# Attention visits of two pairs at a time, on a three-bank PSUM tile, inside a feed-forward matmul stream

## The chip, the cores and the metric

The kernel runs on one core of one Trainium2 chip. The metric is the device time of one execution in microseconds (us). Each engine of the core runs its own list of instructions in order: TensorE (PE, with its weight loads as PEld), VectorE (DVE), ScalarE (ACT), GpSimd (POOL), and SyncE (SP), which here issues nearly all DMA.

## The reference

Eight batches of 576 tokens, eight heads of 64. Heads 0 to 3 attend to the last 32 positions ("local"), heads 4 to 7 to earlier positions with the same remainder by 32 ("strided"). The attention output, 576 x 512 for each batch, goes through a layer norm, two matrices with a ReLU between them, and a residual sum.

```
rel = pos[:, None] - pos[None, :]
mask_local = (rel >= 0) & (rel < 32)
mask_strided = (rel >= 0) & (pos[None, :] % 32 == pos[:, None] % 32)
attn = softmax(where(mask, q @ k.T / 8, -1e9)); attn = attn @ v
x = attn.transpose(0, 2, 1, 3).reshape(B, S, 512)
xn = (x - mean) / sqrt(var + 1e-6) * g_ln
out = x + relu(xn @ w_ch1) @ w_ch2
```

## The kernel before

The feed-forward part sets the rhythm. Tokens come in nine chunks of 512 (one for each batch, and one of the 8 x 64 tokens left over), and the hidden width in 16 slices of 128. One **step** is one chunk and one slice: `ffn1` (L560) runs 12 matmuls of 128x512 into one PSUM bank `ph` (L568, L572), after which ACT makes `hh` (the rounded ReLU, L576) and DVE makes `hl` (what the rounding left, L577); `ffn2` (L581) runs 12 matmuls that add the previous step's `hh` and `hl` into four banks `po` (L587). There are 144 steps, numbered from 0, in the order of `runs`: chunk 0 slices 0 to 7 (steps 0 to 7), chunk 1 (8 to 23), chunk 0 slices 8 to 15 (24 to 31), then chunks 2 to 8 (from step 32, 16 each). Early steps also split the weights into two parts; that ends with step 16.

Attention is worked off in between. A **pair** is two heads of one batch; pairs are numbered 0 to 31, four for each batch, alternately local (even) and strided (odd). A pair needs four pieces of TensorE work: scores `s_piece` (`sp`, L384 or L396), transposes of the weights `p_piece` (`pp`, L429), values `v_piece` (`av`, L443 or L452) and transposes of the result `x_piece` (`px`, L485). The two heads of a pair sit in rows 0-63 and 64-127 of the array, the output rows in column tiles of 32 (local) or 64 (strided); the profile counts two instructions for each such small fp32 matmul. The generator `pieces()` (L771) gives the pieces in order, and each `next(gen)` in the loop over steps is one **visit**: the piece's TensorE work goes between `ffn1` and `ffn2` of that step (or behind `ffn2`, third entry of `slots`). All pieces share one PSUM tile `a` of two banks, so a piece waits until the one before has been read out. From step 24 to 29 each step has two visits, later one, until the pairs are used up.

Between the pieces DVE adds the mask to the scores (`sm`, L403), takes the maximum (`mx`, L410), POOL subtracts it (L419), ACT takes the exponential (L424); after the values DVE divides by the sum of the weights, which comes out of a column of ones beside v (`den`, L458; `xo`, L464), and SP stores `xo`. After the last transposes ACT and DVE split the result into `xh` and `xl` (L502, L504), which `ffn1` of that batch's chunk reads. `turn()` (L764) has DVE transpose the next pair's q and k from `raw` (L361, L366) and SP load the raw rows of the pair after; it stands at the end of a step.

From step 17 on `ps_h` has two banks, which `ffn1` takes in turn (L562). PSUM has eight banks: four for `po`, two for `a`, one for `h`, one that belongs first to `ps_r` and from then on to `h`.

Of the kernel before, what the change touches and what calls it, by code (L numbers as in the profile page):

```python
# [20 lines left out]
def kernel(  # L21
# [46 lines left out]
    ps_r_ctx = ExitStack()  # L68
    ps_r = ps_r_ctx.enter_context(tc.tile_pool(name="ps_r", bufs=1, space=bass.MemoryType.PSUM))

# [107 lines left out]
    class Split:  # L178
# [44 lines left out]
        def column_mean(self, apart=False):  # L223
            if apart:
                self.mean = bank(f"cm{self.f}")[:, 0:P]
            else:
                self.mean = ps_h[0].tile([P, CH], F32, tag="h", name=f"cm{self.f}")[:, 0:P]
            nc.tensor.matmul(self.mean, mean, self.w[0][:, 0:P], start=True, stop=True)
# [18 lines left out]
    banks = [(ps_a, "a")]  # L247
    n_bank = [0]

    def bank(name):  # L250
        pool, tag = banks[n_bank[0] % len(banks)]
        n_bank[0] += 1
        return pool.tile([P, 1024], F32, tag=tag, name=name)

# [9 lines left out]
    class Pair:  # L264
# [45 lines left out]
        def t_rows(self):  # L310
            self.qt, self.kt = (qt_l, kt_l) if self.local else (qt_s, kt_s)
            ps = bank(f"t{self.id}").rearrange("p (c x) -> p c x", c=NR)
            pool, tag = ((ps_r, "r"), (ps_h[0], "h"))[self.local]
# [60 lines left out]
        def s_scores(self):  # L374
            ps = bank(f"sp{self.id}")
            nt = self.nt
            if self.local:
                w, mask = 64, mask_l
                sp = halves(ps, nt, w)
# [9 lines left out]
            else:  # L389
                w, mask = GS, mask_s  # L390
                sp = halves(ps, nt, w)
                for g in range(2 * NS):
                    t, c = divmod(g, 2)
                    for h in range(2):
# [4 lines left out]
                            start=True, stop=True, tile_position=(64 * h, 64 * c))  # L399

            self.sm = sms[int(self.local)]
            sm = self.sm[:, 0:nt, :, 0:w].rearrange("p t h x -> p h t x")
            nc.vector.tensor_tensor(  # L403
                out=sm, in0=sp, in1=mask.unsqueeze(1).unsqueeze(1).broadcast_to([P, 2, nt, w]),
                op=ALU.add)
            if self.local:
# [28 lines left out]
        def v_piece(self):  # L435
# [11 lines left out]
            else:  # L447
# [17 lines left out]
                out=xo[:, 0:nt].rearrange("p t h d -> p h t d"), in0=av[:, :, :, 0:D],  # L465
                in1=den.unsqueeze(3).broadcast_to([P, 2, nt, D]), op=ALU.mult)
            xov = xo.rearrange("p t h d -> p t (h d)")
            self.xov = xov
            if self.local:
                x_b = xd_l[self.b]  # L470
                nc.sync.dma_start(x_b[0:CH, cs].rearrange("(t p) c -> p t c", p=P), xov[:, 0:NT])
                nc.sync.dma_start(x_b[CH:S, cs], xov[0:REST, NT])
            else:
                x_b = xd_s[self.b].rearrange("(t c s) d -> c s t d", c=2, s=GS)
                for c in range(2):
                    nc.sync.dma_start(x_b[c, :, :, cs], xov[64 * c:64 * c + GS, 0:nt])

        def x_piece(self):

            xh, xl = x_t(self.b)  # L480
            cc = self.h0 // 2
            px = bank(f"px{self.id}")
            nt = NT if self.local else NS
            for t in range(nt):
                nc.tensor.transpose(px[:, P * t:P * (t + 1)], self.xov[:, t], ident)  # L485
            if self.local:
# [16 lines left out]
            for src, dst in parts:  # L503
                nc.vector.tensor_tensor(  # L504
                    out=dst(xl), in0=src, in1=dst(xh).bitcast(F32), op=ALU.subtract)

    def split_x(hi, lo, src):
# [49 lines left out]

    n_ffn1 = [0]

    def ffn1(c, f):  # L560
        xh, xl = xt[c]
        ph = ps_h[n_ffn1[0] % len(ps_h)].tile([P, CH], F32, tag="h", name=f"ph{c}_{f}")  # L562
        n_ffn1[0] += 1
        w1h, w1l = (w1s[f][:, i].rearrange("p (c f) -> p c f", c=NCC) for i in range(2))
# [104 lines left out]
    act, dve = nc.scalar.copy, nc.vector.tensor_copy  # L669
    idle = ps_h[0].tile([P, CH], F32, tag="h", name="idle")  # L670
    for i in range(12):
# [88 lines left out]
    def turned(i):  # L760
        if i < NP:
            todo.append(i)
# [8 lines left out]
    def pieces():  # L771

        pairs[NHP].p_piece()
        yield
        for i in range(NHP, NP):
            late = i == 2 * NHP - 1
            if i + 1 < NP and not late:
                pairs[i + 1].s_piece()
                if i + 2 != 2 * NHP:
                    turned(i + 2)  # L780
                yield
            pairs[i].v_piece()
            if i + 2 < NP:
                pairs[i + 2].load_v()
            yield
            if i + 1 < NP and not late:
                pairs[i + 1].p_piece()
                yield
            pairs[i].x_piece()
            if late:  # L790
                turned(i + 1)
            yield
            if late:
                pairs[i + 1].s_piece()
                turned(i + 2)
                yield
                pairs[i + 1].p_piece()
                yield

    gen = pieces()  # L800
    runs = [Run(0, 0, SPLIT), Run(1, 0, NFC), Run(0, SPLIT, NFC)]
# [21 lines left out]
    load = LOADED  # L823
    single = True

# [9 lines left out]
    for n, (r, f) in enumerate(steps):  # L835
        if f == r.f0:
            r.open()
        if load < NFC:
            w_load(load)
            load += 1  # L840
        if single and n > NFC and old is None:
            single = False
            ps_r_ctx.close()
            ps_h.append(ctx.enter_context(
                tc.tile_pool(name="ps_h1", bufs=1, space=bass.MemoryType.PSUM)))
        second = list(range(NT)) if prev is not None else []
        h = ffn1(r.c, f)
        if new and n:
            new.low(0)
# [38 lines left out]
        if old:  # L888
            old.two_parts(1)
        turn()  # L890
        following = prepare(n + 1)
# [48 lines left out]
```

## Time and profile before

| what | us |
|---|---|
| median of 3 runs (967.85, 967.9, 970.51) | 967.9 |
| the profiled execution | 971.69 |
| its span, first to last instruction | 969.9 |
| TensorE matmuls busy | 932.8 (96%) |
| VectorE busy | 388.5 (40%) |
| ScalarE, GpSimd busy | 222.2, 142.8 |

The busy share of TensorE counts matmuls that overlap, each as long as it is in flight, so it says that the engine hardly ever stands empty, not how much of it is needed. What a piece of work costs is read from the distance between two steps. The granted clock is the share of full speed that TensorE was given.

### The profile page before, as it was taken

How to read it: one execution, taken by the hardware profiler on the slowest of the kernel's cores; microseconds unless marked ns; L12 is line 12 of the kernel's file. 1: busy time of each engine (PE TensorE's matmuls, PEld its weight loads, DVE VectorE, ACT ScalarE, POOL GpSimd, SP SyncE). 2: the span in 40 equal slices, each digit the busy share in tenths (PEclk: the TensorE clock that was granted, in tenths of full speed). 3: DMA queues.
4: the chain of work that ended last, by engine and by line, in shares of the span. 5: the costliest groups of instructions: out<-in, count | busy, mean ns of one | idle time of the engine just before them, and what ended most of it. 6: DMA issues, size and time to landing. Idle time of an engine off the chain costs nothing.

```text
span 969.9 us, 19085 instructions
## 1 busy us (share of the span) xinstructions
PE 932.8 (96%) x8176; PEld 762.2 (79%) x8176; DVE 388.5 (40%) x681; ACT 222.2 (23%) x374; POOL 142.8 (15%) x180
## 2 busy tenths in 40 slices
PE   7678899999999999999999999999999999999996
PEld 6556688887788888888888888888888888888885
DVE  3557556444653344433443243335432331122112
ACT  2345557312121212121111121112111111110100
POOL 3246538410100000000100010001000000000000
PEclk8889999999999999999999999999999999999998
DMA  9986771143653233323342434243411121002001
GB/s 200 229 190 173 212 209 59 32 100 89 145 116 81 58 67 75 95 51 72 73 103 52 83 73 105 52 83 73 105 27 36 47 75 46 0 1 87 1 1 43
DMA packets 231971, 82.83 MB, mean 85 GB/s; under 512 B 184656, under 2 KB 222672, under 8 KB 231888
## 3 DMA queue, kind: packets, MB, share of 16 engines
q1 hardware_dynamic: 231360, 81.63, 36.4%
q8 instruction: 64, 1.05, 0.5%
q14 instruction: 19, 0.16, 0.0%
q10 hardware_dynamic: 528, 0.00, 0.0%
HBM read 61.08 MB, written 20.51 MB: 84 GB/s over the span
## 4 chain that ended last, share of the span: by engine, by line
PE 88%; DVE 4%; ACT 2%; issue 2%; SPq 1%; POOL 1%; DMA 1%; DVEq 0%; POOLq 0%; ACTq 0%
PE po L587 39%; PE ph L568 26%; PE ph L572 13%; PE pp L429 2%; PE px L485 2%; PE sp L396 1%; PE av L452 1%; PE av L443 1%; PE sp L384 1%; PE t L317 1%; DMA rows<-in_k_dram 1%; POOL sm L419 1%; DVE x L634 0%; DVE hl L577 0%; SPq L289 0%
## 5 line engine op out<-in xcount | busy, mean ns | idle before, releaser
L587 PE MATMUL po<-w,hh 128*128 128x512 f32 x1152 | 369.2, 402 | 0.0
L577 DVE SCALAR_TENSOR_TENSOR hl<-ph,hh 128x512 fp32r<-128x512 f32 x144 | 99.6, 691 | 500.4 <-ACT hh L576 500.4
L587 PEld LDWEIGHTS po<-w,hh 128*128 128x128 f32 x1152 | 208.3, 189 | 41.9
L568 PE MATMUL ph<-xh,w 128*128 128x512 f32 x576 | 226.8, 394 | 2.3 <-DVE hl L577 1.8
L587 PE MATMUL po<-w,hl 128*128 128x512 f32 x576 | 226.2, 393 | 0.0
L568 PE MATMUL ph<-xl,w 128*128 128x512 f32 x576 | 225.4, 391 | 0.0
L576 ACT ACTIVATE hh<-ph 128x512 fp32r<-128x512 f32 x144 | 85.9, 597 | 546.6 <-PE ph L572 546.6
L572 PE MATMUL ph<-xh,w 128*128 128x512 f32 x576 | 154.5, 390 | 0.0
L568 PEld LDWEIGHTS ph<-xh,w 128*128 128x128 f32 x576 | 108.9, 189 | 25.5 <-DVE hl L577 2.0
L587 PEld LDWEIGHTS po<-w,hl 128*128 128x128 f32 x576 | 108.5, 188 | 24.7
L568 PEld LDWEIGHTS ph<-xl,w 128*128 128x128 f32 x576 | 108.8, 189 | 22.4
L572 PEld LDWEIGHTS ph<-xh,w 128*128 128x128 f32 x576 | 108.4, 188 | 22.7
L419 POOL TENSOR_TENSOR sm<-sm,mx 128x640 f32<-128x640 f32 (+1 forms) x32 | 40.6, 1270 | 432.6 <-DVE mx L410 428.9
L546 POOL TENSOR_TENSOR rs<-rs,mhalf 128x1 f32<-128x1 f32 x36 | 19.7, 548 | 311.7 <-DVE rs L545 311.7
L424 ACT ACTIVATE sm<-sm 128x640 f32<-128x640 f32 (+1 forms) x32 | 23.8, 743 | 118.3 <-POOL sm L419 118.3
L504 DVE TENSOR_TENSOR xl<-px,xh 128x512 fp32r<-128x512 f32 (+2 forms) x48 | 30.0, 656 | 13.4 <-ACT xh L502 13.4
L429 PE MATMUL pp<-ident,sm 128*128 128x128 f32 x176 | 26.2, 285 | 6.2 <-DVE xo L464 3.6
L429 PEld LDWEIGHTS pp<-ident,sm 128*128 128x128 f32 x176 | 22.0, 147 | 11.7 <-issue 3.5
L502 ACT ACTIVATE xh<-px 128x512 fp32r<-128x512 f32 (+2 forms) x48 | 27.5, 648 | 7.2 <-PE px L485 6.5
L464 DVE TENSOR_TENSOR xo<-av,den 128x640 f32<-128x640 f32 (+1 forms) x32 | 28.5, 891 | 1.1
L432 ACT COPY pt<-pp 128x640 f32<-128x640 f32 (+1 forms) x32 | 23.9, 746 | 20.1 <-PE pp L429 17.7
L410 DVE TENSOR_REDUCE mx<-sm 128x10 f32<-128x640 f32 (+1 forms) x32 | 26.4, 824 | 2.1
(86 smaller groups left out, 601.1 us busy)
## 6 DMA issues: line engine op xcount, KB each, us to landing
s<-in_moe_w_ch_dram SPq DMA_DIRECT2D x32, 512.0 KB
out_dram<-x SPq DMA_DIRECT2D x32, 256.0 KB
raw<-in_q_dram SPq DMA_DIRECT2D x104, 72.0 KB
raw<-in_k_dram SPq DMA_DIRECT2D x104, 72.0 KB
xds<-xo SPq DMA_DIRECT2D x32, 162.0 KB
v_l<-in_v_dram SPq DMA_DIRECT2D x32, 144.0 KB
v_l<-in_v_dram SPq DMA_DIRECT2D x32, 136.0 KB
xdl<-xo SPq DMA_DIRECT2D x16, 256.0 KB
```

The source lines that it names most:

```text
L410: nc.vector.reduce_max(mx[:, :, 0:nt], sm, axis=AX.X)
L419: nc.gpsimd.tensor_tensor(out=sm, in0=sm, in1=mx[:, :, 0:nt].unsqueeze(3).broadcast_to([P, 2, nt, w]), op=ALU.subtract)
L429: nc.tensor.transpose(pp[:, P * t:P * (t + 1)], self.sm[:, t].rearrange("p h x -> p (h x)"), ident)
L432: nc.scalar.copy(out=self.pt[:, 0:self.nt].rearrange("p t x -> p (t x)"), in_=pp[:, 0:P * self.nt])
L464: nc.vector.tensor_tensor(out=xo[:, 0:nt].rearrange("p t h d -> p h t d"), in0=av[:, :, :, 0:D], in1=den.unsqueeze(3).broadcast_to([P, 2, ...
L502: nc.scalar.activation(out=dst(xh), in_=src, func=AF.Copy)
L504: nc.vector.tensor_tensor(out=dst(xl), in0=src, in1=dst(xh).bitcast(F32), op=ALU.subtract)
L568: nc.tensor.matmul(ph, w1h[:, cc], x[:, cc, :], start=(n == 0), stop=False)
L572: nc.tensor.matmul(ph, w1l[:, cc], xh[:, cc, :], start=False, stop=(cc == NCC - 1))
L576: nc.scalar.activation(out=hh, in_=ph, func=AF.Relu)
L577: nc.vector.scalar_tensor_tensor(out=hl, in0=ph, scalar=0.0, in1=hh.bitcast(F32), op0=ALU.max, op1=ALU.subtract)
L587: nc.tensor.matmul(run.po[i], hx[:, cs], w, start=(f == run.f0 and n == 0), stop=(f == run.f1 - 1 and n == 2))
```

## The change

From the third batch on (pair 8), two visits take the place of four. `scores_and_values(pv, p)` puts the values of pair `i` and the scores of pair `i + 1` in one visit; `weights_and_x(px, p)` puts the transposes of the result of pair `i` and of the weights of pair `i + 1` in another. Both use a PSUM tile `b` of three banks; the third comes from `ffn1`, which keeps a single bank `ph`. The two heads of a matmul pair are laid out in different banks.

The sum of the weights is no longer a column beside v but a `reduce_sum` over `sm` on DVE. Empty blocks are left out: 36 small matmuls instead of 40 for a local piece, 22 instead of 24 for a strided one. In exchange the mask addition takes two DVE instructions instead of one, and the division three.

`slots` now gives steps 19 and 21 one visit each, each of steps 24 to 31 one, and from step 32 to 110 every second step one. `turn()` moves, from step 17 on, from the end of the step to right behind `ffn1`. Steps 0 to 16 keep their order.

```diff
-    ps_a = ctx.enter_context(tc.tile_pool(name="ps_a", bufs=1, space=bass.MemoryType.PSUM))
-    ps_h = [ctx.enter_context(tc.tile_pool(name="ps_h", bufs=1, space=bass.MemoryType.PSUM))]
+    ps_h = ctx.enter_context(tc.tile_pool(name="ps_h", bufs=1, space=bass.MemoryType.PSUM))
...
+    def scores_and_values(pv, p):
...
+        for n in range(max(map(len, passes))):
+            both = [x[n] if n < len(x) else [] for x in passes]
+            for k in range(max(map(len, both))):
+                for x in both:
+                    if k < len(x):
+                        dst, at, by, pos = x[k]
+                        nc.tensor.matmul(dst, at, by, start=True, stop=True, tile_position=pos)
+        if p:
+            p.s_max(w, [(P, 0, last, a_s[:, :, :, 0:w]), (64, last, last + 1, b_s[0:64, :, :, 0:w])])
+            p.s_exp()
+        if pv:
...
+            pv.x_store(xo, slice(P * pv.n0, P * (pv.n0 + 1)), whole=False)
+
+    def weights_and_x(px, p):
...
+        k = -n_x % NT
+        for t, src in turns_p[:k] + turns_x + turns_p[k:]:
+            nc.tensor.transpose(ps[:, P * t:P * (t + 1)], src, ident)
+        if px:
+            px.x_parts(ps)
+        if p:
...
+            nc.vector.reduce_sum(p.den, p.smv, axis=AX.X)
...
+    def visits():
+
+        for i in range(2 * NHP - 1, NP):
+            p = pairs[i + 1] if i + 1 < NP else None
+            pv = pairs[i] if i >= 2 * NHP else None
+            scores_and_values(pv, p)
+            turned(i + 2)
+            if pv and i + 2 < NP:
+                pairs[i + 2].load_v()
+            yield
+            weights_and_x(pv, p)
+            yield
...
-            slots[n] = (int(8 < f < 14), 0, 0)
+            slots[n] = (int(f in (11, 13)), 0, 0)
         elif r is runs[2]:
-            slots[n] = (1, 0, int(f < 14))
+            slots[n] = (1, 0, 0)
         elif r.c + 1 < B:
-            slots[n] = (1, 0, 0)
+            slots[n] = (int(f % 2 == 0), 0, 0)
...
-        if single and n > NFC and old is None:
-            single = False
-            ps_r_ctx.close()
-            ps_h.append(ctx.enter_context(
-                tc.tile_pool(name="ps_h1", bufs=1, space=bass.MemoryType.PSUM)))
+        if n == NFC + 1:
+            assert old is None and next(gen, None) is None
+            gen = joint
+            first_ctx.close()
+            banks[:] = [(ctx.enter_context(
+                tc.tile_pool(name="ps_b", bufs=1, space=bass.MemoryType.PSUM)), "b")]
+            n_banks[0] = 3
         h = ffn1(r.c, f)
+        if gen is joint:
+            turn()
```

TensorE's list before, from the second visit of step 26 to the first of step 28: four visits, each between two groups of feed-forward matmuls (left out here). `sp` are scores, `pp` and `px` transposes, `av` values; the x at the end counts the matmuls.

```order
L396 MATMUL sp_3_2872<-kt_s,qt_s 64x54 x24
...
L443 MATMUL av_1_2935<-v_l,pt_1_2825 32x65 x40
...
L429 MATMUL pp_3_2999<-ident,sm_195 128x128 x6
...
L485 MATMUL px_1_3038<-ident,xo_1_2979 128x128 x4
```

The same work after the change, in steps 28 and 29: `sv` is the tile of values and scores, the first row the values, the second the next pair's scores.

```order
L574 MATMUL sv_3_2930<-v_l,pt_1_2882 32x64 x36
L574 MATMUL sv_3_2930<-kt_s,qt_s 64x54 x22
...
L602 MATMUL px_3_3058<-ident,xo_1_2995 128x128 x4
L602 MATMUL px_3_3058<-ident,sm_195 128x128 x6
```

Two column-tile widths (32 and 64) now follow each other with no feed-forward matmul between them, and the two kinds of transposes as well.

DVE's list in step 27 after the change, between the `hl` of that step (first row) and the next (last row): the transposes of q and k, the split, the new sum of the weights with its reciprocal, and the layer norm's statistics.

```order
L682 SCALAR_TENSOR_TENSOR hl_11_2852<-ph_11_2838,hh_11_2851 128x512
L367 STREAM_TRANSPOSE qt_s<-raw_3_2679 128x18x32
L367 STREAM_TRANSPOSE kt_s<-raw_3_2679 128x18x32
L519 TENSOR_TENSOR xl_2700<-px_1_2866,xh_2699 128x30x16
L519 TENSOR_TENSOR xl_2700<-px_1_2866,xh_2699 128x2x16
L611 TENSOR_REDUCE den_1_2884<-sm_196 128x2x5
L612 TENSOR_SCALAR den_1_2884<-den_1_2884 128x2x5
L613 RECIPROCAL den_1_2884<-den_1_2884 128x2x5
L649 BN_STATS st_0_2905<-x_0_2721 128x6
...
L728 SCALAR_TENSOR_TENSOR x_0_2721<-t_0_2724,rs_0_2909,x_0_2721 128x512
L682 SCALAR_TENSOR_TENSOR hl_12_2927<-ph_12_2913,hh_12_2926 128x512
```

Before, the list between the `hl` of steps 25 and 26 held a division by `den` alone; the transposes of q and k stood behind the maximum of the scores, ahead of the next `hl`.

```order
L410 TENSOR_REDUCE mx_1_2737<-sm_196 128x2x5
L366 STREAM_TRANSPOSE qt_s<-raw_3_2426 128x18x32
L366 STREAM_TRANSPOSE kt_s<-raw_3_2426 128x18x32
L577 SCALAR_TENSOR_TENSOR hl_9_2766<-ph_9_2752,hh_9_2765 128x512
L458 TENSOR_SCALAR den_2_2794<-av_2_2769 128x12
L459 RECIPROCAL den_2_2794<-den_2_2794 128x12
L464 TENSOR_TENSOR xo_2_2797<-av_2_2769,den_2_2794 128x2x6x64
L577 SCALAR_TENSOR_TENSOR hl_10_2846<-ph_10_2832,hh_10_2845 128x512
```

## Rows read from the trace of the kernel before

**Rows 1.** The page, part 1: busy us, share of the span, instructions.

```profile
PE 932.8 (96%) x8176; PEld 762.2 (79%) x8176; DVE 388.5 (40%) x681; ACT 222.2 (23%) x374; POOL 142.8 (15%) x180
```

**Rows 2.** Single steps: length, busy PE, PEld, DVE, ACT, POOL (count), granted clock, DMA.

```profile
501.59:508.23 6.64, 6.64 (x105) 5.31 (x104) 2.99 (x5) 0.60 (x1) 0.49 (x1) 1.00 0.01 2
508.23:514.78 6.55, 6.55 (x73) 5.22 (x72) 3.57 (x6) 1.34 (x2) 0.78 (x1) 1.00 0.49 80
514.78:520.82 6.04, 6.04 (x30) 5.01 (x29) 0.69 (x1) 1.18 (x2) 0.00 (x0) 1.00 0.52 118
520.82:526.95 6.13, 6.13 (x31) 5.11 (x30) 1.90 (x3) 1.74 (x3) 0.00 (x0) 1.00 0.00 0
526.95:533.47 6.52, 6.52 (x74) 5.22 (x72) 2.87 (x5) 0.60 (x1) 0.47 (x1) 1.00 0.01 3
533.47:540.12 6.65, 6.65 (x105) 5.31 (x104) 2.54 (x6) 1.34 (x2) 0.82 (x1) 1.00 0.60 101
540.12:546.26 6.14, 6.14 (x31) 5.12 (x30) 0.69 (x1) 1.40 (x2) 0.00 (x0) 1.00 0.81 144
546.26:552.20 5.94, 5.94 (x29) 4.90 (x28) 1.29 (x2) 1.09 (x2) 0.00 (x0) 1.00 0.26 74
...
772.73:778.17 5.44, 5.44 (x25) 4.51 (x24) 1.63 (x4) 0.60 (x1) 0.55 (x2) 1.00 0.00 0
```

**Rows 3.** The same table: steps 17 to 23, 24 to 31, 32 to 108.

```profile
179.30:222.19 42.89, 42.89 (x389) 34.97 (x387) 16.60 (x31) 7.81 (x13) 7.29 (x8) 1.00 0.36 74
222.19:280.43 58.24, 56.08 (x661) 44.77 (x660) 35.25 (x61) 12.07 (x20) 6.53 (x8) 1.00 0.55 122
280.43:767.29 486.86, 486.86 (x4486) 396.32 (x4485) 185.63 (x320) 89.69 (x145) 32.94 (x36) 1.00 0.34 73
```

**Rows 4.** Timeline of PE in step 67, a local score visit: start, length.

```profile
503.41 1.07 PE L572 MATMUL ph<-xh,w 128*128 128x512 f32 x4
504.40 1.04 PE L384 MATMUL sp<-kt_l,qt_l 64*32 64x64 f32 x80
505.37 0.73 PE L587 MATMUL po<-w,hh 128*128 128x512 f32 x2
505.94 0.39 PE L587 MATMUL po<-w,hl 128*128 128x512 f32 x1
```

**Rows 5.** Timeline of PE ahead of step 0: local values, then strided scores.

```profile
27.90 1.04 PE L443 MATMUL av<-v_l,pt 64*32 64x65 f32 x80
28.87 0.34 PE L396 MATMUL sp<-kt_s,qt_s 64*64 64x54 f32 x8
```

**Rows 6.** Timeline of step 29: DVE's statistics, residual and division; PE's second visit.

```profile
262.63 0.63 DVE L541 BATCH_NORM_STATS2 st<-x 128x6 f32<-128x512 f32 x1
...
264.35 0.75 DVE L623 SCALAR_TENSOR_TENSOR x<-t,rs,x 128x512 f32<-128x512 f32 x1 [0.67 <-POOL rs L546]
...
266.07 0.96 DVE L464 TENSOR_TENSOR xo<-av,den 128x768 f32<-128x768 f32 x1
...
267.18 0.74 PE L429 MATMUL pp<-ident,sm 128*128 128x128 f32 x5 [1.76 <-DVE xo L464]
```

**Rows 7.** Groups by line on DVE and POOL: busy us, mean ns, idle before.

```profile
L419 POOL TENSOR_TENSOR sm<-sm,mx 128x640 f32<-128x640 f32 (+1 forms) x32 | 40.6, 1270 | 432.6 <-DVE mx L410 428.9 <-DVE den L458 2.0 <-DMA s<-in_moe_w_ch_dram 1.6
L504 DVE TENSOR_TENSOR xl<-px,xh 128x512 fp32r<-128x512 f32 (+2 forms) x48 | 30.0, 656 | 13.4 <-ACT xh L502 13.4
L410 DVE TENSOR_REDUCE mx<-sm 128x10 f32<-128x640 f32 (+1 forms) x32 | 26.4, 824 | 2.1
...
L366 DVE STREAM_TRANSPOSE qt_s<-raw 128x576 f32<-128x576 f32 x13 | 16.2, 1248 | 0.0
```

**Rows 8.** Timeline of step 8, without a visit, `ph` with one bank.

```profile
129.63 1.07 PE L572 MATMUL ph<-xh,w 128*128 128x512 f32 x4
...
131.42 0.69 DVE L577 SCALAR_TENSOR_TENSOR hl<-ph,hh 128x512 fp32r<-128x512 f32 x1 [2.40 <-ACT hh L576]
...
133.25 0.39 PE L568 MATMUL ph<-xh,w 128*128 128x512 f32 x1
```

More of the change, by code (lines that the diff above doesn't have):

```diff
@@ L399, in s_scores, with s_max @@
                             start=True, stop=True, tile_position=(64 * h, 64 * c))
+            self.s_max(w, [(P, 0, nt, sp)])
+        def s_max(self, w, parts):
+            nt = self.nt
+            mask = mask_l if self.local else mask_s
             self.sm = sms[int(self.local)]
             sm = self.sm[:, 0:nt, :, 0:w].rearrange("p t h x -> p h t x")
[L403 to L405 removed]
+            for n, t0, t1, sp in parts:
+                nc.vector.tensor_tensor(
+                    out=sm[0:n, :, t0:t1], in0=sp,
+                    in1=mask[0:n].unsqueeze(1).unsqueeze(1).broadcast_to([n, 2, t1 - t0, w]),
+                    op=ALU.add)
             if self.local:
@@ L475, in v_piece, with x_parts @@
                 for c in range(2):
-                    nc.sync.dma_start(x_b[c, :, :, cs], xov[64 * c:64 * c + GS, 0:nt])
+                    m = nt - (c and not whole)
+                    nc.sync.dma_start(x_b[c, :, 0:m, cs], xov[64 * c:64 * c + GS, 0:m])
         def x_piece(self):
+            px = bank(f"px{self.id}")
+            for t in range(NT if self.local else NS):
+                nc.tensor.transpose(px[:, P * t:P * (t + 1)], self.xov[:, t], ident)
+            self.x_parts(px)
+        def x_parts(self, px):
             xh, xl = x_t(self.b)
             cc = self.h0 // 2
[L482 to L485, printed above, removed]
             if self.local:
@@ new lines, in weights_and_x @@
+    def weights_and_x(px, p):
+        ps = bank(f"px{p.id if p else px.id}")
+        n_x = 0
+        turns_x, turns_p = [], []
+        if px:
+            n_x = NT if px.local else NS
+            turns_x = [(t, px.xov[:, t]) for t in range(n_x)]
+        if p:
+            turns_p = [(n_x + t, p.sm[:, t].rearrange("p h x -> p (h x)")) for t in range(p.nt)]
+        k = -n_x % NT
+        for t, src in turns_p[:k] + turns_x + turns_p[k:]:
+            nc.tensor.transpose(ps[:, P * t:P * (t + 1)], src, ident)
+        if px:
+            px.x_parts(ps)
+        if p:
+            p.pt = smp.tile([P, NS, P], F32, tag="pt", name=f"pt{p.id}")
+            nc.scalar.copy(out=p.pt[:, 0:p.nt].rearrange("p t x -> p (t x)"),
+                           in_=ps[:, P * n_x:P * (n_x + p.nt)])
+            den = stp.tile([P, 2, NS], F32, tag="den", name=f"den{p.id}", bufs=2)
+            p.den = den[:, :, 0:p.nt]
+            nc.vector.reduce_sum(p.den, p.smv, axis=AX.X)
+            nc.vector.tensor_scalar(p.den, p.den, 1e-9, None, op0=ALU.add)
+            nc.vector.reciprocal(out=p.den, in_=p.den)
@@ L669 @@
     act, dve = nc.scalar.copy, nc.vector.tensor_copy
-    idle = ps_h[0].tile([P, CH], F32, tag="h", name="idle")
+    idle = ps_h.tile([P, CH], F32, tag="h", name="idle")
     for i in range(12):
@@ L771, in pieces @@
     def pieces():
+        last = 2 * NHP - 1
         pairs[NHP].p_piece()
         yield
-        for i in range(NHP, NP):
-            late = i == 2 * NHP - 1
-            if i + 1 < NP and not late:
+        for i in range(NHP, last + 1):
+            if i < last:
                 pairs[i + 1].s_piece()
-                if i + 2 != 2 * NHP:
+                if i + 2 <= last:
                     turned(i + 2)
@@ L782, in pieces @@
             pairs[i].v_piece()
-            if i + 2 < NP:
-                pairs[i + 2].load_v()
+            pairs[i + 2].load_v()
             yield
-            if i + 1 < NP and not late:
+            if i < last:
                 pairs[i + 1].p_piece()
@@ L789, in pieces @@
             pairs[i].x_piece()
-            if late:
+            if i == last:
                 turned(i + 1)
             yield
[L793 to L800, printed above, removed]
+    def visits():
[5 more added lines that the diff above has]
+            if pv and i + 2 < NP:
+                pairs[i + 2].load_v()
+            yield
+            weights_and_x(pv, p)
+            yield
+    gen, joint = pieces(), visits()
     runs = [Run(0, 0, SPLIT), Run(1, 0, NFC), Run(0, SPLIT, NFC)]
@@ L889 @@
             old.two_parts(1)
-        turn()
+        if gen is not joint:
+            turn()
         following = prepare(n + 1)
```

70 lines of the change are left out of this document (59 added, 11 removed).

## The prediction

> **What bounds the kernel now.** I read the page first: TensorE is busy 96% of the span [rows 1]. That says little until one knows what a piece of its work costs, so I cut the steady part into stretches from one step's first feed-forward matmul to the next one's [rows 2]. The reader is to see two things there. A step without a visit takes 5.44 us, which is 24 matmuls at 0.227 us; and a step with a visit takes longer by an amount that belongs to the kind of the visit alone, at a granted clock of 1.00 throughout. In the eight rows in order: local scores 1.20, strided values 1.11, local transposes of weights (5) 0.60, strided transposes of x (6) 0.69, strided scores 1.08, local values 1.21, strided weights (6) 0.70, local x (4) 0.50. I also measured the 77 steps from 32 to 108 as one: 486.86 us, 67.98 above 77 x 5.44, and their busy time equals their length [rows 3]: TensorE waits for nobody there. So the kernel is bound by TensorE's list itself, and a change is worth what it takes out of that list, as long as no other engine becomes late.
>
> The eight prices add up to 7.09 for a local and a strided pair; twelve such couples (pairs 8 to 31) make 85.1 us. Measured above the bare steps are 4.81 (steps 17 to 23), 14.72 (24 to 31) and 67.98 [rows 3], 87.5 together. The 2.4 us between them are stalls, and they lie in steps 24 to 31: their 14 visits cost 12.3 by price and 14.7 by the clock. The largest piece is 1.76 us: the second visit of step 29 needs the PSUM tile of the first, and DVE divides it only from 266.07 to 267.03 [rows 6].
>
> **What a visit's price is made of.** In the local score visit [rows 4] the four last matmuls of `ffn1` start at 503.41, so a fifth would at 503.41 + 4 x 0.227 = 504.32; the first small one starts at 504.40: 0.08 to enter. From there to the first matmul of `ffn2` are 0.97. The first two of `ffn2` take 0.57 where two take 0.454: 0.12 to get going again. That is 1.17 of the 1.20; the other 0.03 are spread over the matmuls behind. Now the two layouts of small tiles. Ahead of step 0 local values are followed at once by strided scores, and the distance is 28.87 - 27.90 = 0.97 [rows 5]: going from tiles of 32 columns to tiles of 64 costs the leading visit what going to a full matmul does, no more.
>
> **The scores-and-values visit.** It holds one local and one strided piece. What goes away is one entry, one getting going and the spread rest, 0.08 + 0.12 + 0.03 = 0.23. Fewer small matmuls: 36 instead of 40 local ones are 8 of 80 instructions at 0.97 / 80 = 0.012 or less, I take 0.08; 22 instead of 24 strided ones, 4 of 48 in some 0.85, 0.06. So 0.37 for each of 23 joint visits, 8.5; the first visit (scores alone) and the last (values alone) save 0.08 and 0.06. Their price is then 2.29 or 2.32 less 0.37, 1.92 to 1.95.
>
> The other direction, tiles of 64 first and 32 behind, has no row. Eleven of the visits have it. Below, the change of layout could cost what rows 5 show; above, a whole exit and entry as at a feed-forward matmul, 0.23 more, so 0 to 2.5 us. I take 0.05 each, 0.5 in all, since every change of layout that has a row costs alike.
>
> The Trainium skill (TensorEngine Tiling (Array Packing), Key Properties) says that switching the tiling mode, not just the tile, drains the engine. It speaks against the change, for a joint visit keeps a switch in its middle: three for two pieces where there were four, not two. Rows 5 agree that the switch is paid, and the 0.97 already holds it; by the rule read strictly (a full stop, priced as another exit and entry) the 0.23 would be lost and the visits would save 3.4 us instead of 8.6.
>
> **The weights-and-x visit.** Four to six transposes cost 0.50 to 0.70: 0.10 for each and 0.10 for the visit [rows 2]. Ten or eleven in one visit cost 1.1 or 1.2, so 23 joint visits save 2.3. Nothing is taken out here but the second switch.
>
> **The stalls of steps 24 to 31.** They get one visit each instead of up to two, so that a tile has the rest of the step to be emptied. I worked DVE's list through with the means of its groups [rows 7] (time from the last start in `ffn1`; a step of 7.36 with joint scores and values, 6.54 or 6.64 with transposes). The tightest place is step 27: `hl` from 1.1 to 1.8, as in rows 8; two transposes of q and k to 4.2; two splits of 0.6 to 5.4; the new sum (as long as the maximum, 0.82, with two small ones 1.3) to 6.7; layer norm statistics, a wait for POOL and the residual, 2.5 (from 262.63 to 265.10 in rows 6), to 9.2. The next `hl` is due at 6.64 + 1.1 = 7.7, so it comes 1.5 late; but in step 28 the next `ffn1` starts only after a visit of 1.9 and `ffn2`, 4.9 after the last start, and `hl` is done at 3.3. Step 28 then ends DVE's list at about 8.7 where `hl` is due at 8.5, and the tail is gone by step 31. There `xl` of pair 11 is done at 5.4, and `ffn1` of step 32 reads it, as its eighth matmul, at 1.2 + 2.95 + 7 x 0.227 = 5.7. No stall is left, so 2.4 saved; the margin at this last place is 0.3 us.
>
> **What is added, and what hides it.** DVE gets the sum (0.82 a pair), a second mask addition and two more divisions (some 0.2 each): 1.5 x 24 pairs, 36 us of its time, beside 185.63 busy in the 486.86 of steps 32 to 108 [rows 3], where visits stand in every second step. Every wait of TensorE on it has the rest of two steps. `turn()` now sits ahead of the visit's DVE work, but behind `hl`, and in the visit-free step after the scores: 2.4 us there delay nothing. POOL and ACT do what they did, in the same chain: scores done some 2.1 after the last start, mask and maximum of about 0.9 each, POOL's 1.27 [rows 7] to 5.2; the transposes come at 7.4 at the earliest, which leaves 2.2 for ACT's exponential. On SP the same loads and stores, a DMA each; q and k's raw rows are asked for right behind the turn, as before.
>
> **One bank for `ffn1`.** Now each `ffn1` waits until `hl` of the step before has read the bank. Step 8 ran like that: the last start is 129.63 + 3 x 0.227 = 130.31, `hl` ends at 132.11, the next `ffn1` starts at 133.25 and the step lasts 5.44 [rows 8]. So the wait has 1.1 us of cover in a step without a visit, 2.3 with transposes, 3.0 with scores and values. Cost nothing, and the price of DVE being late by more is that excess.
>
> **Sum.** 8.5 + 0.1 + 2.3 + 2.4 - 0.5 = 12.8. The profiled execution, 971.69 with 1.8 outside its 969.9 of span, would come to 958.9. It is 3.8 above the median, as one of the three timed runs is 2.6 above; what is taken out lies in the steady part and is the same in both, so the median goes from 967.9 to 955.1. I predict **955**.
>
> **Rivals.**
> - *The switch within a visit costs a whole exit and entry.* For it: one direction has no row; against it rows 5, though that is one instance, and the engine stops behind its eighth instruction. Both directions: 23 x 0.23 = 5.3, of which 0.5 is counted: 959.8. The second alone: 957.
> - *The dense steps stall still.* DVE has 35.25 us in 58.24 of steps 24 to 31 now and would have 40 in 56. If the margin of 0.3 breaks, in steps 27 to 32, 1 to 3 us stay: 956 to 958.
> - *The switch is cheaper than rows 5 say*, or small matmuls of the second piece are already queued when it comes: up to 0.13 each, 952.
> - *The single bank turns into the bound (slower).* DVE would have to be late, in each of the 38 visit-free steps from 32 to 108, by so much that the lost time passes 12.8 + 2.9 us: `hl` 1.1 + 0.42 = 1.5 later than in rows 8. The mechanism would be `turn()`: if raw rows come late, DVE stands at the transposes, and the next `hl` behind them. They end at 4.2, `hl` is due at 5.44 + 1.1 = 6.5, and the step behind has a visit of transposes with a cover of 2.3, so raw rows must be 2.3 + 2.3 = 4.6 us late before TensorE loses anything. They are asked for four steps (25 us) ahead, and DVE never waited there: idle 0.0 [rows 7]. At 7 us late at each of 20 turns, 48 us lost: 1003.
>
> **How the numbers follow.** The forecast with its bounds (953.5 to 956.5) gets 0.55; the costlier switch 0.14; stalls left 0.15; the cheaper switch 0.07; the single bank 0.05; the rest, 0.04, is a new wait that I don't see, of any size. The low end takes in the cheaper switch: 952. The high end takes in the costlier one with a little of the stalls: 960.5. Faster or slower counts from 0.3%, 2.9 us, about what runs of this kernel differ by. Slower needs the single bank or an unseen wait, 0.05; within 0.3% are milder forms of the two, 0.05; faster 0.90.
>
> **What would show it.** Steps with scores and values of 7.35 to 7.4, with transposes 6.54 and 6.64, without a visit 5.44; steps 24 to 31 at about 55.8 us instead of 58.24; between the last small matmul of one piece and the first of the other no more than at a visit's end. Wrong would be: `ffn1` waiting for `hl` in the waits of TensorE, steps without a visit above 5.44, or a joint visit of 2.15 or more.

## The result, and the profile after

| | before | after |
|---|---|---|
| median of four runs each, us | 967.88 (967.41 to 970.51) | 957.44 (953.01 to 958.45) |
| profiled execution | 971.69 | 957.88 |
| its span | 969.9 | 956.1 |

The ratio is 0.9878, with a 95% interval of 0.9858 to 0.9898. In a second measurement the changed kernel ran five times more, beside eleven runs of the kernel before: 0.9881 [0.9858, 0.9905]. The prediction, 955 in a range of 952 to 960.5, held, and so did its sign. What its sum is made of did not hold in every term.

Part 1 of the page of the changed kernel, beside [rows 1]:

```profile
PE 922.0 (96%) x7888; PEld 761.7 (80%) x7888; DVE 410.8 (43%) x777; ACT 224.4 (23%) x374; POOL 143.0 (15%) x180
```

TensorE's share has not moved: from step 17 on it is still never idle, as the rows below show, it only has less to do. VectorE has 22 us more of work than before.

The table by stretches of the changed kernel (columns as in [rows 2]). The first two rows are steps 24 to 31 and 17 to 111, each as one. Then steps 27 to 30, and a step without a visit.

```profile
216.81:272.95 56.14, 56.14 (x700) 46.48 (x698) 38.06 (x76) 13.56 (x21) 7.30 (x8) 1.00 0.69 141
176.97:769.77 592.80, 592.80 (x5318) 490.51 (x5316) 264.19 (x517) 113.95 (x181) 48.40 (x54) 1.00 0.36 75
...
238.19:244.88 6.69, 6.69 (x36) 5.67 (x35) 3.12 (x5) 2.48 (x4) 0.50 (x1) 1.00 0.46 111
244.88:252.28 7.40, 7.40 (x141) 6.01 (x140) 6.56 (x17) 1.29 (x2) 1.17 (x2) 1.00 0.72 139
252.28:258.85 6.57, 6.57 (x35) 5.55 (x34) 4.70 (x10) 2.25 (x4) 1.23 (x2) 1.00 0.95 192
258.85:266.26 7.41, 7.41 (x141) 6.01 (x140) 5.84 (x16) 1.10 (x2) 1.31 (x2) 1.00 0.72 142
280.35:285.79 5.44, 5.44 (x26) 4.50 (x24) 4.33 (x7) 1.35 (x2) 0.47 (x1) 1.00 0.91 177
```

The same table of the kernel before, steps 17 to 111 as one:

```profile
179.30:783.61 604.31, 602.15 (x5605) 489.57 (x5604) 242.19 (x421) 111.36 (x181) 48.40 (x54) 1.00 0.35 76
```

These two rows, 604.31 and 592.80, are the result in one number: 11.5 us came out of the steady part. The profiled executions differ by 13.8; the other 2.3 are the start of step 17, at 179.30 before and 176.97 after, and are not the change's. In 13 profiles of this study, of kernels with the same order of work up to there, step 17 starts anywhere from 173.86 to 179.30: from 174.08 to 179.30 in the four with the order of the kernel before, from 173.86 to 178.94 in the nine with the changed one. So nearly all of the spread between runs lies ahead of the change, and the experiments below are read from the start of step 17 to that of step 112.

Every busy time in the rows of after equals its length: the stall of steps 24 to 31, 58.24 long with 56.08 busy in [rows 3], is gone. The visits themselves, in the timeline of TensorE in steps 28 to 31:

```profile
246.69 1.07 PE L677 MATMUL ph<-xh,w 128*128 128x512 f32 x4
247.69 0.97 PE L574 MATMUL sv<-v_l,pt 64*32 64x64 f32 x72
248.59 0.91 PE L574 MATMUL sv<-kt_s,qt_s 64*64 64x54 f32 x44
249.43 0.73 PE L692 MATMUL po<-w,hh 128*128 128x512 f32 x2
250.00 0.39 PE L692 MATMUL po<-w,hl 128*128 128x512 f32 x1
...
254.09 1.08 PE L677 MATMUL ph<-xh,w 128*128 128x512 f32 x4
255.01 0.60 PE L602 MATMUL px<-ident,xo 128*128 128x128 f32 x4
255.45 0.82 PE L602 MATMUL px<-ident,sm 128*128 128x128 f32 x6
256.02 0.71 PE L692 MATMUL po<-w,hh 128*128 128x512 f32 x2
...
261.67 0.92 PE L574 MATMUL sv<-v_s,pt 54*64 54x64 f32 x44
262.51 0.97 PE L574 MATMUL sv<-kt_l,qt_l 64*32 64x64 f32 x72
263.41 0.73 PE L692 MATMUL po<-w,hh 128*128 128x512 f32 x2
```

Read it as the prediction read [rows 4]. In step 28 a fifth `ffn1` matmul would start at 246.69 + 4 x 0.227 = 247.60, and the first small one starts at 247.69: 0.09 to enter. Local values take 0.90, strided scores 0.84 (two counted instructions to a matmul, so x72 are 36). Two `ffn2` matmuls take 0.57 instead of 0.454: 0.12 to get going. There is one entry and one getting going for two pieces. Step 30 has the other direction, 0.84 and 0.90: the same two streams, 1.74 in sum. In step 29 the transposes are entered for 0.01 only (255.01 against 254.09 + 0.91), and their own starts lie 0.11 apart.

### The profile page after: what moved, and what is told of

Its sections match the earlier page's. It is cut to its first block, busy times and chain, and to the rows that moved or that the text cites. A ratio compares the mean times of both kernels' runs of the same rounds, so it can differ in the third digit from the quotient of the medians.

```text
span 956.1 us, 18593 instructions
## 1 busy us (share of the span) xinstructions
PE 922.0 (96%) x7888; PEld 761.7 (80%) x7888; DVE 410.8 (43%) x777; ACT 224.4 (23%) x374; POOL 143.0 (15%) x180
## 4 chain that ended last, share of the span: by engine, by line
PE 92%; ACT 2%; DVE 2%; issue 1%; POOL 1%; DMA 1%; SPq 0%; DVEq 0%; ACTq 0%; POOLq 0%
PE po L692 41%; PE ph L673 27%; PE ph L677 13%; PE sv L574 4%; PE px L602 3%; PE t L318 1%; DMA rows<-in_k_dram 1%; PE pp L437 1%; PE px L494 0%; ACT xh L517 0%; ACT s L188 0%; POOL sm L427 0%; PE av L460 0%; ACT w L242 0%; PE cm L228 0%
## 5 line engine op out<-in xcount | busy, mean ns | idle before, releaser
L692 PE MATMUL po<-w,hh 128*128 128x512 f32 x1152 | 363.4, 397 | 0.0
L692 PEld LDWEIGHTS po<-w,hh 128*128 128x128 f32 x1152 | 210.8, 188 | 42.6
L197 DVE SCALAR_TENSOR_TENSOR p<-s,p 128x512 uint32<-128x512 uint32 x32 | 22.1, 692 | 9.6 <-ACT p L193 9.6
L739 DVE SCALAR_TENSOR_TENSOR x<-po,rs,x 128x512 f32<-128x512 f32 x36 | 24.5, 738 | 3.1 <-PE po L692 2.8
L243 POOL TENSOR_TENSOR w<-wg,w 128x512 fp32r<-128x512 f32 x16 | 20.7, 1297 | 31.4 <-ACT w L242 31.4
L649 DVE BATCH_NORM_STATS2 st<-x 128x6 f32<-128x512 f32 x36 | 24.0, 667 | 1.0 <-DMA x<-xds 1.0
```

Source lines behind the costliest of these rows:

```text
L692: nc.tensor.matmul(run.po[i], hx[:, cs], w, start=(f == run.f0 and n == 0), stop=(f == run.f1 - 1 and n == 2))
L739: nc.vector.scalar_tensor_tensor(out=x, in0=self.po[i], scalar=rs, in1=x, op0=ALU.mult, op1=ALU.add)
```

## The experiments

Eleven kernels. Unless it says otherwise a kernel is the changed kernel with the edit shown; `...` at an end stands for lines of the edit that are left out.

**1. Full blocks again.** The joint visit with as many small matmuls as before, to part the two reasons why it is cheaper.

```diff
-        return ([(divmod(j, 4), STR) for j in range(NB)] if p.local
-                else [(divmod(g, 2), 64) for g in range(NG)])
+        return ([(divmod(j, 4), STR) for j in range(4 * NL)] if p.local
+                else [(divmod(g, 2), 64) for g in range(2 * NS)])
```

> The changed kernel with the empty blocks put back (40 and 24 small matmuls instead of 36 and 22). Theory (a joint visit saves 0.14 by fewer matmuls and the rest by the entry that is left out): steps with scores and values go from 7.40 to about 7.54, and 23 of them add 3.2 us; nothing else moves. Rival (the joint visit saves only by its counts): they go to 7.73, 7.6 us in all. A second rival, that the count costs nothing because the instructions overlap: 7.40.

One run took 958.25. Steps 28 and 30, in the table by stretches, and then the visit of step 28 in the timeline:

```profile
243.12:250.62 7.50, 7.50 (x154) 6.10 (x152) 6.67 (x17) 1.29 (x2) 1.27 (x2) 1.00 0.57 115
...
257.19:264.70 7.51, 7.51 (x153) 6.09 (x152) 5.85 (x16) 1.09 (x2) 1.33 (x2) 1.00 0.78 137
```

```profile
245.93 1.04 PE L574 MATMUL sv<-v_l,pt 64*32 64x64 f32 x80
246.90 0.92 PE L574 MATMUL sv<-kt_s,qt_s 64*64 64x54 f32 x48
247.75 0.72 PE L692 MATMUL po<-w,hh 128*128 128x512 f32 x2
```

The steps are 0.10 longer (7.50 and 7.51 against 7.40 and 7.41), not 0.14. The two streams account for 0.08 of it: 0.97 for 80 counted instructions (0.90 for 72) and 0.85 for 48 (0.84 for 44). So four empty strided instructions are worth 0.01, where the prediction had given them 0.06. The other 0.02 stand in `ffn2`, which takes 2.87 here (247.75 to 250.62) and 2.85 in the changed kernel (249.43 to 252.28). Experiment 11 finds the same 2.87 with nothing put back, so the six small matmuls are worth 0.08 to a visit. What is left of the saving, some 0.25, belongs to the joining.

**2. Scores and values apart again.** The scores go behind the first six `ffn2` matmuls of the same step; work and buffers stay.

```diff
+        n_v = pv.nt if pv else 0
         for n in range(max(map(len, passes))):
+            if n == n_v:
+                yield
...
```

> The changed kernel with the values of a joint visit where they are and the next pair's scores behind the first six matmuls of ffn2, in the same step and the same PSUM tile, so that only the meeting of the two is undone. Theory (meeting saves one entry and one getting going): steps with scores and values go from 7.40 to 7.60 to 7.63, 23 of them add 4.6 to 5.3 us. Rival (the switch of layout in the middle costs as much as leaving and entering): 7.40, nothing added.

963.03 over nine runs, against 968.72 of the kernel before on that chip: 0.9944 [0.9924, 0.9964]. From step 17 to 112 it takes 598.56, 5.8 more than the changed kernel; joint steps are 7.61 and 7.64, 0.21 and 0.23 more (0.19 and 0.21 more than in the execution of experiment 11), and a few steps without a visit, of up to 5.59, make the rest. The timeline shows where:

```profile
247.09 0.97 PE L577 MATMUL sv<-v_l,pt 64*32 64x64 f32 x72
247.99 0.73 PE L697 MATMUL po<-w,hh 128*128 128x512 f32 x2
...
249.56 0.91 PE L577 MATMUL sv<-kt_s,qt_s 64*64 64x54 f32 x44
250.40 0.73 PE L697 MATMUL po<-w,hh 128*128 128x512 f32 x2
```

Six matmuls at 0.227 are 1.36; from 247.99 to 249.56 are 1.57. The 0.21 between them are one getting going and one entry more. Values take 0.90 whether scores or `ffn2` follow, and scores 0.84 whether `ffn2` or values lie ahead: inside the joint visit the change of layout adds nothing to the two streams.

**3. Transposes apart again, first try.** The result's transposes first, the other weights' transposes behind six `ffn2` matmuls, with ACT and DVE reading the result out of the tile in between.

```diff
-        for t, src in turns_p[:k] + turns_x + turns_p[k:]:
+        for t, src in turns_p[:k] + turns_x:
             nc.tensor.transpose(ps[:, P * t:P * (t + 1)], src, ident)
         if px:
             px.x_parts(ps)
+        yield
+        for t, src in turns_p[k:]:
+            nc.tensor.transpose(ps[:, P * t:P * (t + 1)], src, ident)
...
```

> The changed kernel with the x transposes of a joint visit (and the weight transposes that fill their bank) where they are, and the other weight transposes behind the first six matmuls of ffn2. Theory after the result (a transpose costs 0.109 and a visit 0.05 to 0.07): steps with ten go from 6.573 to about 6.63, with eleven from 6.687 to 6.75, 1.4 us in all. Rival (0.10 for a visit, as the prediction had it): 6.67 and 6.79, 2.3 us.

A miss: 985.16, with steps of 7.07 and 7.87. The waits of TensorE from 200 to 800 us have one row (engine and line, what is waited for, us in total, times, longest), and the timeline of step 38 shows one of them:

```profile
PE px L607 <- DVE xl L519: 18.8, 23, 2.3
```

```profile
328.56 0.55 PE L607 MATMUL px<-ident,sm 128*128 128x128 f32 x3 [0.96 <-DVE xl L519]
```

The second half waits for VectorE to have read the first out of the same tile. So this kernel measured a wait that it brought in itself, and nothing of what a visit costs.

**4. The same, without that wait.** Nothing is read out until the second half is written.

```diff
+        n, half = 1, len(turns_x) + k if px and p else n_x or p.nt
         for t, src in turns_p[:k] + turns_x + turns_p[k:]:
             nc.tensor.transpose(ps[:, P * t:P * (t + 1)], src, ident)
+            if n == half:
+                yield
+            n += 1
         if px:
             px.x_parts(ps)
...
```

> Changed kernel, with the transposes of a joint visit in two halves as in the earlier split (the second half behind the first six matmuls of ffn2), but with nothing read out of the tile before the second half is written, so that the half has no wait. It costs what a visit of transposes costs beside its transposes. By the changed kernel's steps, where a joint visit saved 0.067 and 0.046: 6.63 to 6.64 with ten transposes and 6.73 to 6.75 with eleven. By the prediction's 0.10: 6.67 and 6.79. Rival (full-size matmuls between the halves cost nothing to enter, and the saving was something else): 6.57 and 6.69 as they are.

958.45 in one run. The joint steps are 6.61 and 6.71, 0.036 and 0.023 more than 6.573 and 6.687, which the changed kernel has in both its profiles. That lies between the rival, which expected nothing, and the lowest other value, and is farthest from the prediction's 0.10. The timeline of step 29:

```profile
254.89 0.60 PE L603 MATMUL px<-ident,xo 128*128 128x128 f32 x4
255.24 0.71 PE L696 MATMUL po<-w,hh 128*128 128x512 f32 x2
...
256.72 0.81 PE L603 MATMUL px<-ident,sm 128*128 128x128 f32 x6
257.29 0.71 PE L696 MATMUL po<-w,hh 128*128 128x512 f32 x2
```

With `ffn2` behind them four transposes take 0.35 to the next start; with six more transposes behind them they took 0.44 (255.01 to 255.45 in the changed kernel). Getting `ffn2` going costs 0.12 (255.24 to 256.72 are 1.48, six matmuls 1.36). By these starts 0.09 of it is time of the fourth transpose, 0.44 less 0.35, which a joint visit pays as well. So a visit of transposes has next to no fixed price to save.

**5. The kernel before with one bank for `ffn1`.**

```diff
-            ps_h.append(ctx.enter_context(
-                tc.tile_pool(name="ps_h1", bufs=1, space=bass.MemoryType.PSUM)))
```

> The kernel before with a single bank for ffn1 throughout, nothing else changed. Theory (hl is done 1.1 us and more before the bank is needed): every step as before, 5.44 without a visit and the eight prices unchanged, the dense steps 24 to 31 within 0.5 us of 58.24, the time the same within 0.3%. Rival (the bank was worth something that the visits' gain now hides): TensorE waits for hl, 3 us or more in all.

968.59 over ten runs against 968.72: 0.9999 [0.9982, 1.0016]. From step 17 to 112 it takes 604.32, with two banks 604.31. The bank that the change takes from `ffn1` was worth nothing.

**6 and 7. `hl` made late, with one bank and with two.** Two extra maxima over `hh` ahead of `hl` in every second step from 33 to 109: in the changed kernel these are the steps without a visit. Kernel 7 is the kernel before with the same edit.

```diff
         nc.scalar.activation(out=hh, in_=ph, func=AF.Relu)
+        if now[0] in range(33, 110, 2):
+            for _ in range(2):
+                dm = stp.tile([P, 1], F32, tag="dm", name=f"dm{c}_{f}_{_}", bufs=1)
+                nc.vector.reduce_max(dm, hh.bitcast(F32), axis=AX.X)
...
```

> The changed kernel with two extra DVE instructions (a maximum over hh, some 0.67 each, result unused) ahead of hl in the 39 visit-free steps 33, 35, ... 109, so that hl ends 1.35 to 1.4 later. Theory (single bank, cover of 1.1 to 1.15 us): these steps go from 5.44 to 5.65 to 5.75, 8 to 12 us in all, and TensorE's waits name hl. Rival (as much cover as with two banks): 5.44, nothing.

> The kernel before, two banks for ffn1, with the same two extra DVE instructions ahead of hl in the same steps 33, 35, ... 109. Theory (ffn2 of the next step is the first to need hl, 3.9 us later or more): every step as before, nothing added. Rival (hl is needed as early as with one bank): these steps 0.1 to 0.3 longer where the visit is short.

974.29 for the changed kernel with the edit, 968.64 for the kernel before with it, 969.31 for the kernel before itself on that chip. Steps 33 and 34 of the changed kernel with the edit, in the table, and then in the timeline:

```profile
282.32:287.99 5.67, 5.60 (x25) 4.32 (x23) 4.53 (x8) 1.35 (x2) 0.47 (x1) 1.00 0.91 183
287.99:294.72 6.73, 6.73 (x34) 5.67 (x35) 3.81 (x7) 2.00 (x3) 0.00 (x0) 1.00 0.90 220
```

```profile
285.93 1.41 DVE L687 TENSOR_REDUCE dm<-hh 128x1 f32<-128x512 f32 x2 [1.11 <-ACT hh L683]
287.26 0.68 DVE L688 SCALAR_TENSOR_TENSOR hl<-ph,hh 128x512 fp32r<-128x512 f32 x1
...
287.53 0.39 PE L698 MATMUL po<-w,hl 128*128 128x512 f32 x1
287.99 0.50 PE L675 MATMUL ph<-xh,w 128*128 128x512 f32 x1
288.33 0.40 PE L675 MATMUL ph<-xl,w 128*128 128x512 f32 x1
```

`hl` ends at 287.94, and the first `ffn1` matmul, due at 287.53 + 0.23 = 287.76, starts at 287.99. The step without a visit is 0.23 longer, as the cover of 1.1 lets expect. The step behind it is longer too, by 0.13 to 0.16, which was not expected: the first matmul after the wait takes 0.34 to the next start instead of 0.227. From step 17 to 112 it takes 607.25, 14.45 more than the changed kernel, where 8 to 12 were expected. With two banks nothing is added (604.28). So the single bank has a price, and it needs `hl` some 1.1 us late to show: `hl` ends 5.62 after the start of step 33, 4.30 in the changed kernel, and of these 1.32 us 0.23 are lost.

The list of TensorE's waits was expected to name `hl`, and it has no row at all from 285 to 760 us. So an empty list of waits does not show that nothing waited; the lengths of the steps do.

**8. The kernel before without layer norm work in the dense steps.** It leaves out the statistics and the residual sum of chunk 0 in steps 27 to 30 (a constant scales chunk 0, and its first partial sum is not added).

```diff
+                if not self.first:
+                    r[1] = mhalf
+                    return
                 r[1] = x_scale(x, f"{self.c}_{i - 2}")
```

> The kernel before without the layer norm statistics and the residual's first half in steps 27 to 30 (chunk 0 is scaled by a constant and its first partial sum left out, so chunk 0's output isn't the reference's). Theory (the stall of step 29 is DVE's list: the division of the first visit comes late behind the statistics and residuals of steps 28 and 29): step 29 falls from 9.10 to 7.2 to 7.5, step 25 keeps its 7.74, steps 24 to 31 fall from 58.24 to 56.3 to 56.7. Rival (two visits on one PSUM tile in a step stall by themselves): step 29 stays above 8.5.

964.74 in one run. Steps 24 to 31, 25 and 29 in the table by stretches:

```profile
216.97:273.49 56.52, 56.09 (x661) 44.76 (x660) 28.63 (x44) 12.08 (x20) 4.27 (x4) 1.00 0.58 126
223.97:231.71 7.74, 7.35 (x82) 5.66 (x78) 6.49 (x10) 1.23 (x2) 1.26 (x1) 1.00 0.54 151
253.34:260.73 7.39, 7.35 (x83) 5.66 (x78) 5.96 (x9) 1.22 (x2) 1.27 (x1) 1.00 0.87 157
```

Step 29 falls from 9.10 to 7.39, and step 25, which holds no such work, stays at 7.74, 0.4 of it not busy. The waits of TensorE in the kernel before from 222 to 281 us have one row (waited for, us in total, times, longest):

```profile
PE pp L429 <- DVE xo L464: 2.2, 2, 1.8
```

So 1.7 us of the stall were the layer norm's work in VectorE's list, as [rows 6] had been read. The 0.4 of step 25 are a wait for the division as well; what delays it there no run took out.

**9. Narrow strided scores.** A strided block has 54 rows of q, but 64 columns of the array were loaded for it, 10 of them with rows of the next block.

```diff
-                        (dst[m * c:m * (c + 1), 0:w], p.qt[r, step * i:step * i + m],
+                        (dst[m * c:m * c + min(m, step), 0:w],
+                         p.qt[r, step * i:step * i + min(m, step)],
...
```

> The changed kernel with 54 instead of 64 stationary columns in each strided score matmul (the ten spare output rows are left out, and the mask is added in three parts instead of two). In the profile before, strided values with 65 moving columns and strided scores with 54 took the same time, so it isn't the moving side. If the load of the stationary columns sets the pace: the strided half of a visit goes from 0.65 to 0.55, steps from 7.40 to 7.31, 23 visits with a strided half, 12 of them scores: 1.1 us in all. If the pace is a fixed one for a tile of 64: 7.40, no change.

953.52 in one run, 591.60 from step 17 to 112. Steps with strided scores fall by 0.10 to 7.30, those with strided values stay at 7.41. The same 44 instructions, in the timeline:

```profile
245.39 0.81 PE L575 MATMUL sv<-kt_s,qt_s 64*54 64x54 f32 x44
246.12 0.74 PE L699 MATMUL po<-w,hh 128*128 128x512 f32 x2
```

0.73 by these starts instead of 0.84, and 0.10 by the steps: the theory of the loaded columns holds for the scores.

**10 and 11. Both narrow, beside the changed kernel once more.** The strided values lose their 10 columns too.

```diff
-                        (dst[m * c:m * (c + 1)], pv.pt[64 * h:64 * h + rows, t, m * c:m * (c + 1)],
+                        (dst[m * c:m * c + min(m, rows)],
+                         pv.pt[64 * h:64 * h + rows, t, m * c:m * c + min(m, rows)],
...
```

> Changed kernel, with 54 instead of 64 stationary columns in the strided scores and in the strided values too; the mask addition takes three DVE instructions for a strided pair and the division five. With the scores alone narrowed, a visit of local values and strided scores fell from 7.400 to 7.300 and the other kind stayed at 7.407. Theory (64-column tiles are paced by their stationary columns, 0.10 us for 22 matmuls): now the steps with strided values and local scores fall too, from 7.407 to 7.30, the last visit (strided values alone) from 6.51 to 6.41, and from step 17 to step 112 it takes 590.4, 2.4 less than the changed kernel. Rival (the gain belongs to the scores, whose moving side was 54 columns wide already, and the values with 65 moving columns are paced by those): 7.407 stays, 591.6. Rival on the other side: two more divisions make DVE late in steps 24 to 31, which then take over 56.1.

> The changed kernel as it is, to stand beside the version with narrow strided tiles on the same chip. Steps as before: with values and scores 7.40 and 7.41, with transposes 6.57 and 6.69, without a visit 5.44; from step 17 to step 112 592.8 us.

954.56 over six runs, 0.9864 [0.9839, 0.9889] of the kernel before; the changed kernel beside it 955.38 over five, 0.9881 [0.9858, 0.9905]. The intervals overlap, so the whole time does not tell the two apart. From step 17 to 112 it is 591.25 against 593.32. Of the narrow one, steps 28 and 30 in the table, and the visit of step 30 in the timeline:

```profile
245.73:253.05 7.32, 7.32 (x141) 5.92 (x140) 6.46 (x14) 1.29 (x2) 0.55 (x1) 1.00 0.69 136
259.62:267.00 7.38, 7.38 (x142) 5.97 (x140) 5.82 (x14) 1.09 (x2) 1.32 (x2) 1.00 0.93 136
```

```profile
262.44 0.88 PE L576 MATMUL sv<-v_s,pt 54*54 54x64 f32 x44
263.25 0.97 PE L576 MATMUL sv<-kt_l,qt_l 64*32 64x64 f32 x72
264.15 0.73 PE L703 MATMUL po<-w,hh 128*128 128x512 f32 x2
```

The changed kernel beside it, step 28 in the table, and the first matmuls of its `ffn2`:

```profile
242.42:249.84 7.42, 7.42 (x141) 6.01 (x140) 6.58 (x17) 1.29 (x2) 1.18 (x2) 1.00 0.78 157
...
246.97 0.72 PE L692 MATMUL po<-w,hh 128*128 128x512 f32 x2
```

It had 7.42 and 7.43 in steps 28 and 30 in that execution, some 0.02 more than in its first profile, from the same code. The streams of small matmuls are as long as there; the 0.02 stand in `ffn2` behind them, 2.87 here (246.97 to 249.84) and 2.85 in the first profile. Step 30 of the narrow kernel has 2.85 (264.15 to 267.00). So its 0.05 to 0.06 against 7.43 hold some 0.02 that are not the columns', and the streams are to be compared: strided scores gain 0.10 again, strided values 0.03 (0.84 to 0.81). The last visit, strided values alone, falls from 6.51 to 6.47. That is about a third of what the theory had. Neither the theory nor its rival holds for the values; their moving side has 64 columns here, not the 65 that the expectation names, which is the kernel before.

The four streams would fit a pace set by the longer side of the matmul (loaded 64 and moving 54: 0.84; 64 and 64: 0.84; 54 and 54: 0.73; 54 and 64: 0.81), up to 0.03. That is not shown: the scores have 64 rows and the values 54, and no run varied the moving side alone. The rival of late divisions falls: steps 24 to 31 take 55.88.

## Why the prediction was right, and which terms were off

The mechanism was right: TensorE's list is the bound, the change takes entries and small matmuls out of it and ends a stall of VectorE's making, and nothing new became late. Of 12.8 us in the sum, 11.5 came (604.31 to 592.80). Term by term:

| term | predicted | measured | how |
|---|---|---|---|
| joint scores and values, second direction included | 8.5 - 0.5 = 8.0 | 7.65 | 12 x 0.326 + 11 x 0.340 |
| first and last visit | 0.1 | 0.09 | 6.587 and 6.514 for 6.64 and 6.55 |
| joint transposes | 2.3 | 1.31 | 12 x 0.067 + 11 x 0.046 |
| stalls of steps 24 to 31 | 2.4 | 2.46 | what is left of 11.51 |

- **The number.** 955 was the median of three runs less 12.8; less 11.5 it would have been 956.4. The four runs gave 957.44, and they spread by 5.4 us, as much as the start of step 17 does in the profiles, so the last 1 us can't be told from chance. One price is added up wrong, 1.11 and 1.20 are 2.31 and not 2.32; no term of the sum rests on it.
- **The entry, 0.23: right.** Experiment 2 puts it back and finds 0.19 to 0.23; what is left after experiment 1 is some 0.25.
- **Fewer matmuls, 0.14: too much.** Experiment 1 finds 0.08. The step "22 instead of 24 strided ones, 4 of 48 in some 0.85, 0.06" failed: it took the mean of a stream as the price of its last members. They cost 0.01. That the whole term of joint scores and values came so close is partly luck: this was 1.3 us too much in 23 visits, and the 0.5 taken off for the second direction and a slightly larger entry made up for most of it.
- **Transposes, "0.10 for each and 0.10 for the visit": the largest miss of the table, 1.0 us.** The split was fitted to prices of 0.50, 0.60 and 0.70. Inside a visit the starts lie 0.11 apart, so a piece of four to six costs 0.44 to 0.66 by its members alone, and little is left for the visit: 0.02 to 0.04 in experiment 4. The pieces of the kernel before cost 0.067 or 0.046 more than the joint ones; what makes the rest of that, 0.02 to 0.03, was not tried.
- **The change of layout inside the visit, 0.05 in the direction without a row: not found.** Steps of 7.400 and 7.407 are 0.326 and 0.340 below the prices of their parts, so the second direction costs no more than the first. The Trainium skill (TensorEngine Tiling (Array Packing), Key Properties) says that a switch of mode drains the engine. The price by that rule, another exit and entry, would have left a saving of some 0.08 to a visit; the measured 0.33 and experiment 2 speak against so high a price here.
- **The dense steps: right, with more room than thought.** `hl` of step 28 was to be 1.5 late and the tail gone by step 31; it was 0.7 late and the tail gone by step 29. The last place, `xl` of pair 11 ahead of step 32, had a margin of 0.75 where 0.3 was worked out:

```profile
249.15 0.68 DVE L682 SCALAR_TENSOR_TENSOR hl<-ph,hh 128x512 fp32r<-128x512 f32 x1
...
255.90 0.69 DVE L682 SCALAR_TENSOR_TENSOR hl<-ph,hh 128x512 fp32r<-128x512 f32 x1 [1.13 <-ACT hh L681]
...
272.67 1.11 DVE L519 TENSOR_TENSOR xl<-px,xh 128x480 fp32r<-128x480 f32 x2
...
274.53 0.39 PE L673 MATMUL ph<-xl,w 128*128 128x512 f32 x1
```

  The last `ffn1` matmuls of steps 28 and 29 start at 247.37 and 254.77, so `hl` stands 1.78 and 1.13 behind them (1.06 to 1.13 where nothing holds it up). `xl` is ready at 273.78 for a matmul at 274.53.
- **VectorE's added work, 36 us: too much, and without effect.** From step 17 to 112 it was busy 264.19 instead of 242.19, 22.0 more. The new sum came as expected (24 of 0.82, 19.6). A second mask addition and two more divisions, "some 0.2 each", cost less than 0.2 together, because the parts are shorter: the three divisions of a pair keep VectorE busy for 1.00 (24.1 in all) where one took 0.89, the two mask additions for 0.89 (21.3) where one took 0.82.
- **One bank for `ffn1`, cost nothing: right.** Experiment 5 finds no price, and no step without a visit is above 5.44 once step 17 is past. Experiments 6 and 7 show that the rival's mechanism exists and needs a lateness that this kernel doesn't have.
- **The rivals.** The costlier switch and the remaining stall are ruled out by the steps; of the cheaper switch, up to 0.13 a visit, at most 0.02 came: with 0.08 for the matmuls, 0.25 is left of the saving where 0.23 was worked out.

## What to carry to other kernels

On a saturated engine, a merge of two small pieces saves the fixed part of one, so measure that part: two sizes of the same piece give the price of a member, and a fit through pieces of different kinds does not. The price of leaving members out is that of the last ones, not the mean of the stream. Where one execution spreads by 5 us ahead of the change, compare the stretch that the change touches: in two executions of the changed kernel it came to 592.80 and 593.32, and it told apart versions that the whole time did not. Inside a step, compare the starts of the pieces, since a step of the same code moved by 0.02.

## What the runs showed of the hardware

- The streams of small strided matmuls got shorter by 0.10 when 54 instead of 64 columns were loaded with 54 moving, and by 0.03 with 64 moving (experiments 9 and 10).
- A full-size matmul that waited for VectorE cost its wait, and the step behind took 0.13 to 0.16 longer (0.34 from that matmul to the next start instead of 0.227; experiment 6).
- Four transposes took 0.35 with `ffn2` behind them and 0.44 with other transposes behind them (experiment 4 and the changed kernel).
- The same code gave joint steps of 7.40 in one execution and 7.42 in another, every visit of a kind alike within each; the streams of small matmuls were as long, and `ffn2` behind them took 2.85 and 2.87.
